# A K stage issued from a timetable instead of a loop: one pipelined stage of an attention and feed-forward kernel, reordered on four engines

## The chip, the cores and the metric

The kernel runs on one core of one Trainium2 chip. The metric is the device time of one execution in microseconds (us). Each execution is timed by itself; "fast" is the undisturbed state. The profiled execution of each kernel leaves a trace; its span is about 1.7 us shorter than the time of the same execution (530.5 against 532.15 us for the kernel before). PE is the matmul engine (TensorE), PEld its weight load, DVE the vector engine, ACT the scalar engine, POOL the general-purpose engine, SP the engine that issues the loads and stores here. "Landing" is the moment at which loaded data is there. A "bank" is a part of ps_all, the memory that PE's results go to; it can be written anew once DVE and ACT have read it.

## The reference, cut to what matters

```python
def _A_ref(x, wqkv, wo):                       # x: 1 x 2048 x 576, 32 heads of 18
    qkv = ((x @ wqkv).reshape(B, S, 3, H, Dh)).transpose(2, 0, 3, 1, 4)
    q, k, v = qkv[0], qkv[1], qkv[2]
    phi = lambda t: jnp.where(t > 0, t + 1, jnp.exp(t)) + 1e-6
    pq, pk = phi(q), phi(k)
    kv = jnp.einsum("bhsd,bhse->bhde", pk, v)
    z = jnp.einsum("bhsd->bhd", pk)
    ...                                        # num / den, then @ wo
def _B_ref(x, w_gate, w_up, w_down):
    return (_gelu(x @ w_gate) * (x @ w_up)) @ w_down
xn = _layernorm(x, axis=-1)
return x + _A_ref(xn, A_wqkv, A_wo) + _B_ref(xn, B_w_gate, B_w_up, B_w_down)
```

The sums over tokens in kv and z are taken on PE as a Gram matrix of xn and pk, so that V is never formed.

## The kernel before

The 2048 tokens are 16 tiles of 128. Each tile goes through a pipeline: statistics (mean and variance: DVE, two halves and an aggregate), rstd (one over the square root of the variance; ACT: Ln, then Exp), norm (DVE), five transposes (PE) and their copy (ACT), ten K matmuls in two halves (PE), phi of K (relu and exp on ACT, max on DVE, a sum on POOL), and the Gram matmuls two tiles behind (PE). In these traces each engine takes its instructions in the program's order: in experiment 4 ACT stands still for 0.99 us before one instruction while the input of a later one is ready.

```python
    def ln_rstd(n, cnt=1):
        r = rstd[:, n:n + cnt]
        nc.scalar.activation(out=r, in_=mv[:, n:n + cnt, 1], func=ACT.Ln, bias=eps_ln[:], scale=1.0)
        nc.scalar.activation(out=r, in_=r, func=ACT.Exp, scale=-0.5)
    ...
    for n in range(1, NS):                      # NS = 16, PAIRED = 7, GLAG = 2
        if n > 1:
            k_half(n, 0); k_half(n, 1)
        if n + 1 < NS:
            tp_all(n + 1)                       # ACT copies the transposes
        if n + 2 < NS and (n + 2 < PAIRED or n % 2 == 1):
            ln_rstd(n + 2, min(1 if n + 2 < PAIRED else 2, NS - n - 2))
        if n + 2 < NS:
            ln_norm(n + 2)
        k_read(n, 0); k_read(n, 1); k_finish(n) # relu, max; exp and POOL sum
        ln_stats(2 * (n + 4) + (1 if n < PAIRED - 4 else 2))   # half statistics done so far
        if n >= GLAG:
            g_accumulate(n - GLAG, G_A)
        if n + 2 < NS:
            transposes(n + 2)
        if n in (NS - 2, NS - 1):
            q_unit(...)                         # Q units 0 and 1 between the last K tiles
        ...                                     # loads of x and of later weights
    ...
    for i in range(2, NSC * NCH):               # the other Q units
        q_unit(i)
        if i < 2 + GLAG:
            g_accumulate(NS - GLAG + i - 2, G_A)    # the last two Gram tiles
        ...
```

The first two tiles have a hand-written order ahead of this loop. Q is made in units, each a block of five matmuls followed by its own phi. The phi tiles of K and of the Q units share one pool: three buffers for the exp side, two (phi_a) for the max side. After the Q units come the denominators, and from about 77 us on the feed-forward part, 85% of the time.

Of the kernel before, what the change touches and what calls it, by code (L numbers as in the profile page):

```python
# [8 lines left out]
ACT = mybir.ActivationFunctionType  # L9
# [6 lines left out]
P = 128  # L16
# [23 lines left out]
GLAG = 2  # L40
PAIRED = 7
XW = 642
# [14 lines left out]
def kernel(  # L57
# [139 lines left out]

    ln_done = [0]

    def ln_stats(halves):  # L200

        while ln_done[0] < min(halves, 2 * NS):
            n, a_ = divmod(ln_done[0], 2)
            if a_ == 0:
                stats_t[n] = asmall.tile([P, 2, nc.vector.BN_STATS_DIM], F32, name="stats")
            nc.vector.bn_stats(out=stats_t[n][:, a_, :], in_=x_sb[:, n, a_ * HALF:(a_ + 1) * HALF])
            if a_ == 1:
                nc.vector.bn_aggr(out=mv[:, n, :], in_=stats_t.pop(n)[:])
            ln_done[0] += 1

    def ln_rstd(n, cnt=1):
        r = rstd[:, n:n + cnt]
        nc.scalar.activation(out=r, in_=mv[:, n:n + cnt, 1], func=ACT.Ln, bias=eps_ln[:], scale=1.0)
        nc.scalar.activation(out=r, in_=r, func=ACT.Exp, scale=-0.5)

    def ln_norm(n, dup=None):
        nc.vector.tensor_scalar(  # L217
            out=xn[:, n, 0:D], in0=x_sb[:, n, :], scalar1=mv[:, n, 0:1], scalar2=rstd[:, n:n + 1],
            op0=ALU.subtract, op1=ALU.mult,
        )  # L220
        (dup or nc.gpsimd).tensor_copy(out=xn[:, n, D:640], in_=xn[:, n, 512:D])

# [5 lines left out]

    def tp_copy(n, k0, k1, copy):
        copy(out=xnT[:, k0:k1, n * P:(n + 1) * P], in_=tp_bank[:, k0:k1, :])  # L230

# [18 lines left out]

    def k_read(n, hf):
        if hf == 0:
            k_ea[n] = phi_tiles()
        e, a = k_ea[n]
        hs = slice(hf * HALF, (hf + 1) * HALF)
        src = ps_all[:, k_bank(n, hf), :HALF]
        nc.scalar.activation(out=e[:, hs], in_=src, func=ACT.Relu, scale=-1.0)
        nc.vector.tensor_scalar(
            out=a[:, hs], in0=src, scalar1=0.0, scalar2=EPS_ATT, op0=ALU.max, op1=ALU.add,
        )  # L260

    def k_finish(n):
        e, a = k_ea.pop(n)
        nc.scalar.activation(out=e[:], in_=e[:], func=ACT.Exp, scale=-1.0)  # L264
        nc.gpsimd.tensor_tensor(out=pk[:, n, :], in0=e[:], in1=a[:], op=ALU.add)  # L265
# [10 lines left out]
    def g_accumulate(n, pieces):  # L276
# [10 lines left out]
    G_COPIES = {  # L287
        3: [(0, G_A, 0, acopy), (0, G_A, 1, vcopy), (2, G_A, 0, acopy), (2, G_A, 1, vcopy)],
        5: [(1, G_A, 0, acopy), (2, G_A, 2, vcopy)],
# [3 lines left out]
    }  # L293

    def tp_all(n):
        tp_copy(n, 0, KT, acopy)

    q_next = [0]

# [86 lines left out]


    ln_stats(2)
    ln_rstd(0)
    ln_stats(3)  # L390
    ln_norm(0, nc.vector)
    transposes(0)
    ln_stats(4)
    tp_copy(0, 0, KT, vcopy)
    ln_rstd(1)
    k_half(0, 0)
    ln_norm(1)
    transposes(1)
    ln_stats(6)
    k_half(0, 1)  # L400
    k_read(0, 0)
    tp_all(1)
    ln_rstd(2)
    ln_stats(7)
    k_half(1, 0)
    ln_norm(2)
    k_read(0, 1)
    k_finish(0)
    transposes(2)
    k_half(1, 1)  # L410
    ln_stats(9)


    for n in range(1, NS):

        if n > 1:
            k_half(n, 0)
            k_half(n, 1)
        if n + 1 < NS:
            tp_all(n + 1)  # L420
        if n + 2 < NS and (n + 2 < PAIRED or n % 2 == 1):
            ln_rstd(n + 2, min(1 if n + 2 < PAIRED else 2, NS - n - 2))
        if n + 2 < NS:
            ln_norm(n + 2)
        k_read(n, 0)
        k_read(n, 1)
        k_finish(n)
        ln_stats(2 * (n + 4) + (1 if n < PAIRED - 4 else 2))
        if n >= GLAG:
            g_accumulate(n - GLAG, G_A)  # L430
        if n + 2 < NS:
            transposes(n + 2)
        if n in (NS - 2, NS - 1):
            q_unit(q_next[0])
            q_next[0] += 1
        if n == 2:
            load_x(8, 4)
        elif n == 3:
            load_x(12, 4)
        elif n == 5:  # L440
            load_w(0)
        elif n == 6:
            load_w(2)
        elif n == 7:
            load_wo()
        elif 8 <= n < 8 + NWBUF:
            load_gu(n - 8, 0)
            load_gu(n - 8, 1)

# [7 lines left out]
    for i in range(2, NSC * NCH):  # L457
        if i == 8:
            q_banks = _Ring([2, 3, 4, 5, 6, 7])
        q_unit(i)  # L460
        if i < 2 + GLAG:
            g_accumulate(NS - GLAG + i - 2, G_A)
        for kt, pieces, part, copy in G_COPIES.get(i, ()):
            g_copy(kt, pieces, part, copy)
        if i == 10:
            z_stage()
        if 5 <= i < 13:
            for n in (2 * (i - 5), 2 * (i - 5) + 1):
                g_accumulate(n, G_B)
        if 13 <= i < 13 + NCH:  # L470
            den_mm(0, i - 13, q_banks.next())
        if i == 17:
            kv_stage()
# [163 lines left out]
```

## Time and profile before

| what | kernel before |
|---|---|
| time, median of 3 (range) | 532.59 us (532.07 to 533.6) |
| span of the profiled run, granted clock | 530.5 us, 1.0 |
| K stage and Q units, up to the first feed-forward matmul | 77.66 us |
| feed-forward part, from there to the end | 452.8 us |
| K stage, per tile, tiles 5 to 13 | 2.625 us |

The change touches only the first 77 us, and what it does there is read off the moment at which the first feed-forward matmul starts. The chain of waits is the profile's account of what the last instruction waited for, followed back in time; its columns are start, length, what. That moment stands in the last line here:

```profile
75.47 2.18 PE ps_all L310 x10
77.66 1.40 PE ps_all L505 x11
```

L310 is the last Q unit, L505 the feed-forward part. The other lines of the profile before are in the prediction.

### The profile page before, as it was taken

To read this page: it belongs to the slowest core of one execution; us is meant where nothing else is said; L and a number is where in the kernel's file an instruction comes from. 1 tells how busy PE (TensorE), PEld (TensorE's weight loads), DVE (VectorE), ACT (ScalarE), POOL (GpSimd) and SP (SyncE) were. 2 spreads that over 40 slices of the span, in tenths; PEclk is the share of its full clock that TensorE was granted. 3 is DMA by queue.
4 is the path that set the end of the run, shared out by engine and by line. 5 is a ranking of instruction groups with operands and counts; after the bars stand their busy time and mean duration, and the time that the engine had idled before them with its cause. 6 is when DMAs were issued, how large, how long until landed. Compare 5 with 4: busy or idle time off the path is not lost.

```text
span 530.5 us, 10752 instructions
## 1 busy us (share of the span) xinstructions
PE 522.6 (99%) x4532; PEld 314.3 (59%) x4532; DVE 248.7 (47%) x408; ACT 152.5 (29%) x288; POOL 70.3 (13%) x83
## 2 busy tenths in 40 slices
PE   7999999999999999999999999999999999999997
PEld 5887666444467754444477744444677544445775
DVE  7885666783338613333368233333485143333101
ACT  6887783323330003323200022323100132322000
POOL 4666542110002100000012000000021000000000
PEclk9999999999999999999999999999999999999999
DMA  8910006898510025555400055555100345540000
GB/s 283 248 30 1 1 2 184 261 270 267 143 39 12 23 78 153 148 150 157 135 12 12 12 153 162 146 157 153 49 22 13 94 143 158 155 135 1 12 12 22
DMA packets 98810, 55.85 MB, mean 105 GB/s; under 512 B 5322, under 2 KB 98378, under 8 KB 98762
## 3 DMA queue, kind: packets, MB, share of 16 engines
q1 hardware_dynamic: 98762, 55.17, 36.2%
q8 instruction: 35, 0.57, 0.4%
q14 instruction: 13, 0.11, 0.1%
HBM read 52.79 MB, written 2.36 MB: 104 GB/s over the span
## 4 chain that ended last, share of the span: by engine, by line
PE 95%; SPq 2%; DVE 1%; ACT 1%; issue 0%; DMA 0%
PE ps_all L505 51%; PE ps_all L576 27%; PE ps_all L310 4%; PE ps_all L581 4%; PE ps_all L280 4%; PE ps_all L238 3%; PE ps_all L227 1%; SPq L166 1%; PE ps_all L370 1%; SPq L168 0%; SPq L169 0%; DMA x_sb<-in_A_x_dram 0%; ACT xnT L230 0%; DVE xn L217 0%; PE ps_all L358 0%
## 5 line engine op out<-in xcount | busy, mean ns | idle before, releaser
L505 PE MATMUL ps_all<-xnT,wg 64*128 64x512 bf16 x1152 | 274.1, 377 | 0.0
L505 PE MATMUL ps_all<-xnT,wu 64*128 64x512 bf16 x1152 | 272.6, 377 | 0.9 <-SPq L514 0.3
L549 DVE TENSOR_TENSOR hT<-ps_all,gl 128x512 bf16<-128x512 f32 x144 | 99.6, 692 | 168.9 <-ACT gl L548 168.7
L548 ACT ACTIVATE gl<-ps_all 128x512 f32<-128x512 f32 x144 | 86.0, 597 | 316.7 <-PE ps_all L505 294.9
L505 PEld LDWEIGHTS <-wu 64*128 64x128 bf16 x1152 | 106.9, 94 | 70.9 <-SPq L514 8.7
L505 PEld LDWEIGHTS <-wg 64*128 64x128 bf16 x1152 | 107.0, 94 | 66.7 <-issue 0.3
L576 PE MATMUL ps_all<-wd_sb,hT 128*128 128x288 bf16 x1152 | 146.6, 286 | 0.0
L576 PEld LDWEIGHTS <-hT 128*128 128x128 bf16 x1152 | 112.2, 98 | 31.5 <-issue 1.9
L384 DVE RECIPROCAL den_sb<-den_sb 126x128 f32<-126x128 f32 (+1 forms) x80 | 68.3, 911 | 0.5
L385 POOL TENSOR_TENSOR pqT<-pqT,den_sb 126x512 bf16<-126x512 bf16 (+3 forms) x25 | 24.1, 965 | 301.5 <-DVE den_sb L384 298.2
L584 DVE TENSOR_TENSOR res<-ps_all,x_sb 128x288 bf16<-128x288 f32 x32 | 14.6, 458 | 88.3 <-PE ps_all L581 88.3
L505 PE MATMUL ps_all<-xnT,wr 64*128 64x512 bf16 x288 | 55.9, 377 | 0.0
L581 PE MATMUL ps_all<-m_sb,pqT 126*128 126x288 bf16 (+1 forms) x160 | 24.9, 286 | 0.0
L505 PEld LDWEIGHTS <-wr 64*128 64x128 bf16 x288 | 14.6, 94 | 17.4 <-issue 1.1
L310 PE MATMUL ps_all<-xnT,wqkv_sb 128*126 128x512 bf16 (+1 forms) x100 | 24.4, 380 | 0.0
L265 POOL TENSOR_TENSOR hT<-phi_e,phi_a 128x576 bf16<-128x576 f32 x16 | 22.5, 1404 | 8.9 <-ACT phi_e L264 4.9
L280 PE MATMUL ps_all<-hT,xn 128*128 128x288 bf16 (+3 forms) x192 | 23.6, 266 | 0.0
L238 PE MATMUL ps_all<-wqkv_sb,xnT 128*128 128x288 bf16 x160 | 22.4, 286 | 0.8 <-DVE xnT L230 0.6
L280 PEld LDWEIGHTS <-xn 128*128 128x128 bf16 (+1 forms) x192 | 18.2, 101 | 4.5
L320 POOL TENSOR_TENSOR pqT<-phi_e,phi_a 126x512 bf16<-126x512 f32 (+1 forms) x14 | 17.7, 1268 | 15.5 <-DVE phi_a L318 11.8
L581 PEld LDWEIGHTS <-pqT 126*128 126x128 bf16 (+1 forms) x160 | 15.5, 97 | 4.1
L238 PEld LDWEIGHTS <-xnT 128*128 128x128 bf16 x160 | 15.0, 98 | 4.5 <-DVE xnT L230 0.8
(58 smaller groups left out, 200.6 us busy)
## 6 DMA issues: line engine op xcount, KB each, us to landing
wg<-in_B_w_gate_dram SPq DMA_DIRECT2D x72, 256.0 KB, 2.9
wu<-in_B_w_up_dram SPq DMA_DIRECT2D x72, 256.0 KB, 3.4
wd_sb<-in_B_w_down_dram SPq DMA_DIRECT2D x12, 432.0 KB, 4.5
wr<-in_B_w_gate_dram SPq DMA_DIRECT2D x72, 32.0 KB, 2.7
wr<-in_B_w_up_dram SPq DMA_DIRECT2D x72, 32.0 KB, 3.1
out_dram<-res SPq DMA_DIRECT2D x15, 144.0 KB, 1.8
x_sb<-in_A_x_dram SPq DMA_DIRECT2D x3, 576.0 KB, 6.6
wqkv_sb<-in_A_wqkv_dram SPq DMA_DIRECT2D x2, 576.0 KB, 9.2
```

The costliest lines, as they stand in the source:

```text
L238: nc.tensor.matmul(ps_all[:, k_bank(n, hf), :HALF], lhsT=xnT[:, kt, n * P:(n + 1) * P], rhs=wqkv_sb[:, kt, D + hf * HALF:D + (hf + 1) * HALF],
L265: nc.gpsimd.tensor_tensor(out=pk[:, n, :], in0=e[:], in1=a[:], op=ALU.add)
L280: nc.tensor.matmul(ps_all[:m, b, col:col + w], lhsT=xn[:, n, j0:j0 + m], rhs=pk[:, n, d0:d0 + w], start=(n == 0 and col == 0), stop=(n == ...
L310: nc.tensor.matmul(ps, lhsT=wqkv_sb[:, kt, q0:q0 + rows], rhs=xnT[:, kt, cs], start=(kt == 0), stop=(kt == KT - 1),)
L320: nc.gpsimd.tensor_tensor(out=pqT[:rows, c, cs], in0=e, in1=a, op=ALU.add)
L384: nc.vector.reciprocal(out=d[:, h:h + P], in_=d[:, h:h + P])
L385: nc.gpsimd.tensor_tensor(out=pqT[:rows, c, cols], in0=pqT[:rows, c, cols], in1=d, op=ALU.mult)
L505: return nc.tensor.matmul(self.outs[i], lhsT=self.lhs(i, rows, kt), rhs=self.rhs(i, rows, kt), start=start, stop=stop, skip_group_check=True,)
L548: nc.scalar.activation(out=gl[:], in_=ps_all[:, b[0], :], func=ACT.Gelu_apprx_tanh)
L549: nc.vector.tensor_tensor(out=hT[:, GUB * k + i, :], in0=ps_all[:, b[1], :], in1=gl[:], op=ALU.mult)
L576: nc.tensor.matmul(acc, lhsT=hT[:, f, j * P:(j + 1) * P], rhs=wd_sb[:, f, hs], start=(f == 0), stop=False,)
L581: nc.tensor.matmul(acc, lhsT=pqT[:rows, c, ts_], rhs=m_sb[:rows, c, hs], start=False, stop=(c == NCH - 1),)
```

## The change

The loop is replaced by a table. Each step of a tile has a list of times, the first four tiles with times of their own, later tiles 2.5 us apart; all steps are sorted by time and issued in that order. Three things come with it. No rstd is paired any more. Inside a tile the second K half stands after the next tile's transposes, and the halves' statistics, relus and maxes are issued one by one. At the end, Q unit 0 stands ahead of K of tile 15, and the last two Gram tiles, the copies that read them and the second Gram pass move one Q unit later. The times in the table fix only an order; nothing waits for a clock.

```diff
-PAIRED = 7
...
+    TILE = 2.5
+    STEPS = [
+        (lambda n: ln_half(n, 0), [3.02, 3.99, 6.44, 7.41, 9.44]),
+        (lambda n: ln_half(n, 1), [3.51, 4.48, 6.93, 7.90, 9.93]),
+        (ln_rstd, [4.14, 5.11, 7.56, 10.12, 11.84]),
+        (ln_norm, [4.96, 5.69, 8.38, 10.77, 12.80]),
...
+        (transposes, [5.66, 6.57, 9.14, 11.53, 13.62]),
+        (tp_copy, [6.07, 6.98, 9.56, 12.27, 14.12]),
+        (lambda n: k_half(n, 0), [6.86, 8.09, 10.30, 13.01, 15.56]),
+        (lambda n: k_half(n, 1), [7.47, 9.43, 10.91, 13.91, 16.46]),
...
+        (lambda n: k_max(n, 0), [8.72, 10.41, 12.44, 14.61, 17.27]),
+        (lambda n: k_max(n, 1), [9.08, 11.11, 13.28, 15.60, 17.84]),
+        (k_exp, [8.73, 11.12, 13.29, 15.61, 18.10]),
+        (k_add, [9.59, 11.73, 14.01, 16.29, 19.88]),
+    ]
+    G_AT = [11.82, 14.53, 17.07, 19.62, 22.16]
+    todo = [(at(times, n), step, n) for n in range(NS) for step, times in STEPS]
+    todo += [(at(G_AT, n), lambda n: g_accumulate(n, G_A), n) for n in range(NS - GLAG)]
+    todo += [(at(STEPS[7][1], NS - 1) - 0.01, q_unit, 0), (at(G_AT, NS - GLAG) - 0.01, q_unit, 1)]
+    for _, step, n in sorted(todo, key=lambda x: x[0]):
+        step(n)
...
-        if i < 2 + GLAG:
-            g_accumulate(NS - GLAG + i - 2, G_A)
+        if 3 <= i < 3 + GLAG:
+            g_accumulate(NS - GLAG + i - 3, G_A)
```

More of the change, by code (lines that the diff above doesn't have):

```diff
@@ L196, with ln_half, ln_rstd, ln_norm @@
     stats_t = {}
-    ln_done = [0]
-    def ln_stats(halves):
-        while ln_done[0] < min(halves, 2 * NS):
-            n, a_ = divmod(ln_done[0], 2)
-            if a_ == 0:
-                stats_t[n] = asmall.tile([P, 2, nc.vector.BN_STATS_DIM], F32, name="stats")
-            nc.vector.bn_stats(out=stats_t[n][:, a_, :], in_=x_sb[:, n, a_ * HALF:(a_ + 1) * HALF])
-            if a_ == 1:
-                nc.vector.bn_aggr(out=mv[:, n, :], in_=stats_t.pop(n)[:])
-            ln_done[0] += 1
-    def ln_rstd(n, cnt=1):
-        r = rstd[:, n:n + cnt]
-        nc.scalar.activation(out=r, in_=mv[:, n:n + cnt, 1], func=ACT.Ln, bias=eps_ln[:], scale=1.0)
+    def ln_half(n, a_):
+        if a_ == 0:
+            stats_t[n] = asmall.tile([P, 2, nc.vector.BN_STATS_DIM], F32, name="stats")
+        nc.vector.bn_stats(out=stats_t[n][:, a_, :], in_=x_sb[:, n, a_ * HALF:(a_ + 1) * HALF])
+        if a_ == 1:
+            nc.vector.bn_aggr(out=mv[:, n, :], in_=stats_t.pop(n)[:])
+    def ln_rstd(n):
+        r = rstd[:, n:n + 1]
+        nc.scalar.activation(out=r, in_=mv[:, n, 1:2], func=ACT.Ln, bias=eps_ln[:], scale=1.0)
         nc.scalar.activation(out=r, in_=r, func=ACT.Exp, scale=-0.5)
-    def ln_norm(n, dup=None):
+    def ln_norm(n):
         nc.vector.tensor_scalar(
@@ L220, in ln_norm, with ln_dup @@
         )
-        (dup or nc.gpsimd).tensor_copy(out=xn[:, n, D:640], in_=xn[:, n, 512:D])
+    def ln_dup(n):
+        (nc.gpsimd if n else nc.vector).tensor_copy(out=xn[:, n, D:640], in_=xn[:, n, 512:D])
     tp_bank = ps_all[:, 7, :].bitcast(BF16).rearrange("p (k t) -> p k t", t=P)
@@ L227, in transposes, with tp_copy @@
             nc.tensor.transpose(tp_bank[:, kt, :], xn[:, n, kt * P:(kt + 1) * P], ident[:])
-    def tp_copy(n, k0, k1, copy):
-        copy(out=xnT[:, k0:k1, n * P:(n + 1) * P], in_=tp_bank[:, k0:k1, :])
+    def tp_copy(n):
+        copy = acopy if n else vcopy
+        copy(out=xnT[:, :, n * P:(n + 1) * P], in_=tp_bank[:, 0:KT, :])
     def k_bank(n, hf):
@@ L249, with k_relu, k_max, k_exp @@
     k_ea = {}
-    def k_read(n, hf):
+    def k_relu(n, hf):
         if hf == 0:
             k_ea[n] = phi_tiles()
-        e, a = k_ea[n]
         hs = slice(hf * HALF, (hf + 1) * HALF)
-        src = ps_all[:, k_bank(n, hf), :HALF]
-        nc.scalar.activation(out=e[:, hs], in_=src, func=ACT.Relu, scale=-1.0)
+        nc.scalar.activation(out=k_ea[n][0][:, hs], in_=ps_all[:, k_bank(n, hf), :HALF], func=ACT.Relu, scale=-1.0)
+    def k_max(n, hf):
+        hs = slice(hf * HALF, (hf + 1) * HALF)
         nc.vector.tensor_scalar(
-            out=a[:, hs], in0=src, scalar1=0.0, scalar2=EPS_ATT, op0=ALU.max, op1=ALU.add,
-        )
-    def k_finish(n):
+            out=k_ea[n][1][:, hs], in0=ps_all[:, k_bank(n, hf), :HALF],
+            scalar1=0.0, scalar2=EPS_ATT, op0=ALU.max, op1=ALU.add,
+        )
+    def k_exp(n):
+        e = k_ea[n][0]
+        nc.scalar.activation(out=e[:], in_=e[:], func=ACT.Exp, scale=-1.0)
+    def k_add(n):
         e, a = k_ea.pop(n)
-        nc.scalar.activation(out=e[:], in_=e[:], func=ACT.Exp, scale=-1.0)
         nc.gpsimd.tensor_tensor(out=pk[:, n, :], in0=e[:], in1=a[:], op=ALU.add)
@@ L287 @@
     G_COPIES = {
-        3: [(0, G_A, 0, acopy), (0, G_A, 1, vcopy), (2, G_A, 0, acopy), (2, G_A, 1, vcopy)],
+        4: [(0, G_A, 0, acopy), (0, G_A, 1, vcopy), (2, G_A, 0, acopy), (2, G_A, 1, vcopy)],
         5: [(1, G_A, 0, acopy), (2, G_A, 2, vcopy)],
@@ L293 @@
     }
-    def tp_all(n):
-        tp_copy(n, 0, KT, acopy)
-    q_next = [0]
     q_banks = _Ring([7])
@@ L385, in den_norm @@
         nc.gpsimd.tensor_tensor(out=pqT[:rows, c, cols], in0=pqT[:rows, c, cols], in1=d, op=ALU.mult)
-    ln_stats(2)
-    ln_rstd(0)
-    ln_stats(3)
-    ln_norm(0, nc.vector)
-    transposes(0)
-    ln_stats(4)
-    tp_copy(0, 0, KT, vcopy)
-    ln_rstd(1)
-    k_half(0, 0)
-    ln_norm(1)
-    transposes(1)
-    ln_stats(6)
-    k_half(0, 1)
-    k_read(0, 0)
-    tp_all(1)
-    ln_rstd(2)
-    ln_stats(7)
-    k_half(1, 0)
-    ln_norm(2)
-    k_read(0, 1)
-    k_finish(0)
-    transposes(2)
@@ L410 @@
-    k_half(1, 1)
-    ln_stats(9)
-    for n in range(1, NS):
-        if n > 1:
-            k_half(n, 0)
-            k_half(n, 1)
-        if n + 1 < NS:
-            tp_all(n + 1)
-        if n + 2 < NS and (n + 2 < PAIRED or n % 2 == 1):
-            ln_rstd(n + 2, min(1 if n + 2 < PAIRED else 2, NS - n - 2))
-        if n + 2 < NS:
-            ln_norm(n + 2)
-        k_read(n, 0)
-        k_read(n, 1)
-        k_finish(n)
-        ln_stats(2 * (n + 4) + (1 if n < PAIRED - 4 else 2))
-        if n >= GLAG:
-            g_accumulate(n - GLAG, G_A)
-        if n + 2 < NS:
-            transposes(n + 2)
-        if n in (NS - 2, NS - 1):
-            q_unit(q_next[0])
-            q_next[0] += 1
-        if n == 2:
-            load_x(8, 4)
-        elif n == 3:
-            load_x(12, 4)
-        elif n == 5:
-            load_w(0)
-        elif n == 6:
-            load_w(2)
-        elif n == 7:
-            load_wo()
-        elif 8 <= n < 8 + NWBUF:
-            load_gu(n - 8, 0)
-            load_gu(n - 8, 1)
+    TILE = 2.5
@@ new lines @@
+    STEPS = [
[3 more added lines that the diff above has]
+        (ln_norm, [4.96, 5.69, 8.38, 10.77, 12.80]),
+        (ln_dup, [5.43, 6.16, 8.85, 11.24, 13.27]),
+        (transposes, [5.66, 6.57, 9.14, 11.53, 13.62]),
+        (tp_copy, [6.07, 6.98, 9.56, 12.27, 14.12]),
+        (lambda n: k_half(n, 0), [6.86, 8.09, 10.30, 13.01, 15.56]),
+        (lambda n: k_half(n, 1), [7.47, 9.43, 10.91, 13.91, 16.46]),
+        (lambda n: k_relu(n, 0), [7.99, 9.28, 11.56, 13.84, 16.55]),
+        (lambda n: k_relu(n, 1), [8.27, 10.55, 12.83, 15.11, 17.39]),
+        (lambda n: k_max(n, 0), [8.72, 10.41, 12.44, 14.61, 17.27]),
[3 more added lines that the diff above has]
+    ]
@@ new lines, with at @@
+    G_AT = [11.82, 14.53, 17.07, 19.62, 22.16]
+    def at(times, n):
+        return times[n] if n < len(times) else times[-1] + TILE * (n - len(times) + 1)
+    todo = [(at(times, n), step, n) for n in range(NS) for step, times in STEPS]
+    todo += [(at(G_AT, n), lambda n: g_accumulate(n, G_A), n) for n in range(NS - GLAG)]
+    todo += [(at(STEPS[7][1], NS - 1) - 0.01, q_unit, 0), (at(G_AT, NS - GLAG) - 0.01, q_unit, 1)]
+    load_x(8, 4)
+    load_x(12, 4)
+    load_w(0)
+    load_w(2)
+    load_wo()
@@ L451, in g_copy @@
+    for i in range(NWBUF):
+        load_gu(i, 0)
+        load_gu(i, 1)
+    for _, step, n in sorted(todo, key=lambda x: x[0]):
+        step(n)
     def g_copy(kt, pieces, part, copy):
@@ L466 @@
             z_stage()
-        if 5 <= i < 13:
-            for n in (2 * (i - 5), 2 * (i - 5) + 1):
+        if 6 <= i < 14:
+            for n in (2 * (i - 6), 2 * (i - 6) + 1):
                 g_accumulate(n, G_B)
```

## The prediction

> **What bounds the kernel now.** The page's first lines are read first: which engine is busy, and what the chain that ended last is made of.
>
> ```profile
> PE 522.6 (99%) x4532; PEld 314.3 (59%) x4532; DVE 248.7 (47%) x408; ACT 152.5 (29%) x288; POOL 70.3 (13%) x83
> ...
> PE 95%; SPq 2%; DVE 1%; ACT 1%; issue 0%; DMA 0%
> ```
>
> The kernel is TensorE from end to end; the change adds and removes no matmul, so it can only win TensorE gaps. Its busy figure hides small waits, so I read the K stage in two ways. By stretch of time (columns: length, then us of busy time and instruction counts of PE, PEld, DVE, ACT, POOL, then the granted clock, DMA share and GB/s):
>
> ```profile
> 5.00:10.00 5.00, 4.12 (x38) 2.72 (x36) 4.50 (x15) 3.12 (x9) 0.61 (x3) 1.00 0.99 354
> 10.00:15.00 5.00, 3.94 (x40) 3.06 (x38) 4.21 (x12) 4.87 (x13) 3.33 (x5) 1.00 1.06 368
> 15.00:20.00 5.00, 5.00 (x53) 4.28 (x51) 4.62 (x16) 4.80 (x13) 3.28 (x5) 1.00 1.13 219
> 20.00:30.00 10.00, 10.00 (x98) 8.14 (x96) 8.66 (x24) 8.47 (x20) 6.37 (x8) 1.00 0.77 201
> ```
>
> Here PE lacks some 2 us before 15 us, and DVE and ACT are both near full: three engines are almost balanced. From 15 to 20 us there are 53 matmuls in 5 us, from 20 to 30 us only 98 in 10: the steady state got slower although PE still shows as full. The timeline says why. The change to look for is the first instruction that idles:
>
> ```profile
> 20.42 0.21 DVE L208 BATCH_NORM_AGGREGATE mv<-stats 128x2 f32<-128x12 f32 x1
> ...
> 20.67 0.30 ACT L213 ACTIVATE rstd<-mv,eps_ln 128x2 f32<-128x2 f32 x1 [0.42 <-DVE mv L208]
> 21.00 0.21 ACT L214 ACTIVATE rstd<-rstd 128x2 f32<-128x2 f32 x1
> ...
> 21.24 0.43 DVE L217 TENSOR_SCALAR xn<-x_sb,mv,rstd 128x576 bf16<-128x576 bf16 x1 [0.61 <-ACT rstd L214]
> ...
> 21.72 0.40 PEld L227 LDWEIGHTS <-xn 128*128 128x128 bf16 x5 [0.19 <-DVE xn L217]
> ```
>
> From tile 7 on, one rstd serves two tiles, so it waits for the second tile's statistics; ACT, then DVE, then the transposes wait in a row. The first K matmuls of tiles 3, 4, 5, 6, 7, 8, 9 start at 14.36, 16.84, 19.36, 22.12, 24.65, 27.41 and 29.90 us: 2.48 and 2.52 us per tile with single rstds, then 2.76 + 2.53 and 2.76 + 2.49. Over the eight tiles from 5 (19.36) to 13 (40.36) it is 21.00 us, 2.625 each. From tile 13 to the feed-forward part at 77.6 us PE has no gap.
>
> **What the Trainium skill says.** "TensorE: Matmul & The Clock Gate", Back-to-back issue gap, gives N/2.4 + 2.5 ns between warm matmuls, though it warns that streams with weight loads may differ. For one tile that is 5 x 55.8 (transposes) + 10 x 122.5 (K) + (2304 columns / 2.4 + 10 x 2.5) (Gram) = 0.28 + 1.23 + 0.98 = 2.49 us. This trace agrees: the chain of waits has exactly pieces of 0.28, 1.23 and 0.98 us, and single-rstd tiles take 2.49. So 2.49 is the floor per tile and TILE = 2.5 sits on it. "Perfetto Trace Analysis", Optimizing Scalar/DVE Operations, says that grouping into larger operations helps a saturated engine; pairing rstd was that. The trace agrees with the saving (0.30 us for two columns as for one) and shows its price, the wait above. "PSUM — Partial Sum Buffer", PSUM bank collisions, asks for semaphores per bank between readers; the built program has them (each DVE max waits for the ACT relu of the same bank), and the tail below turns on that.
>
> **The change, part by part.**
>
> *Single rstd for tiles 7 to 14.* Four more Ln/Exp pairs, about 0.44 us of ACT each. ACT per tile is then: relu 0.30, relu to exp 0.42, exp 0.59, copy 0.69, Ln to Exp 0.33, Exp 0.11, as issue distances in the timeline around 16 us: 2.44 us, just under 2.49. If PE holds its floor over the eight tiles: 21.00 - 8 x 2.49 = **1.08 us gained**. I trust this most, because tiles 3 to 5 of the kernel before already ran so.
>
> *The first four tiles.* The timetable wants the K matmuls of tile 4 at 15.56 us; before, they stand at 16.84, after one transpose group more (0.28), so at equal work 16.56: 1.0 us on paper. But the new order puts both halves of the statistics of tiles 2 and 3 ahead of norm 2 on DVE, at 6.44 and 7.41, and the landings in the trace are about 6.85 us for x of tile 2 and 8.1 for tile 3 (tile 4's block 9.5). DVE works in order, so I replay it with row durations (statistics 0.41 a half, aggregate 0.16 with its wait, norm 0.43, max 0.41): tile 2's statistics 6.85 to 7.67; tile 3's 8.1 to 8.92; norm 2 at 9.1 (before 8.80); two maxes, tile 4's statistics, one max, norm 3 at 11.7 (before 11.01); norm 4 at 13.9 (before 13.38); norm 5 at 16.1 (before 15.87). On PE: transposes 2 at 9.55, both K halves of tile 2 from 10.85, transposes 3 at 12.2, Gram 0 at 12.6, K of tile 3 at 13.55, then with waits of 0.2 on norm 4 and on the bank, K of tile 4 at about 16.35. The split of K around the transposes fills most of the old 1.06 us hole before tile 3's transposes, and DVE's late start takes most of that back: gain 0.2 by replay, 1.0 by timetable. I take **0.4 us**.
>
> *Q unit 0 ahead of K of tile 15, and the Gram tail.* In the built order the POOL sum of Q unit 0 now stands ahead of the K sum of tile 14, and ACT does Q 0's relu and exp before tile 14's exp. Before:
>
> ```profile
> 46.41 0.60 ACT L317 ACTIVATE phi_e<-ps_all 126x512 f32<-126x512 f32 x1 [1.01 <-PE ps_all L310]
> 47.04 0.63 ACT L319 ACTIVATE phi_e<-phi_e 126x512 f32<-126x512 f32 x1
> ...
> 48.31 1.27 POOL L320 TENSOR_TENSOR pqT<-phi_e,phi_a 126x512 bf16<-126x512 f32 x1 [1.43 <-ACT phi_e L257]
> ```
>
> In the new order the first DVE max of tile 15 waits for that POOL sum (its phi_a buffer is the one Q 0 had; two buffers). Count from the first K matmul of tile 14: Q 0 on PE at 2.45; its relu 1.35 later as before (46.41 against 45.06), 3.8; max 0.70 later, 4.5 to 5.2; POOL sum 5.35 to 6.6; tile 15's first max 6.65 to 7.1. Q unit 2 wants that bank on PE at 6.8 (0.60 + 0.28 + 0.60 + 0.98 + 1.08 + 1.23 + 0.98 + 1.08): a new wait of 0.3 us, or 0.7 if the POOL sum is again 0.4 us later than its inputs (48.31 against 47.80 + 0.14). Gram 15 needs POOL's sum of tile 15: Q 1's sum 8.9 to 10.15, then 1.40 to 11.55, against PE's arrival at 11.4 with the tail one Q unit later (without that shift at 10.3, a wait of over 1 us; so the shift is needed by the new order and gains nothing against before). **Cost 0.5 us.**
>
> *The loads* stand in the same order on their queue: 0.
>
> Sum: 1.08 + 0.4 - 0.5 = 1.0 us of 532.6. After the stage PE has no gap for the rest of the run, so what is won at 50 us arrives at the end whole.
>
> **The rivals.**
>
> *The timetable works as written:* landings early enough, no new wait in the tail: 1.0 + 1.08 = 2.1 us, 530.5. For it: the times fit the engines' row durations. Against: the landings above and the POOL order.
>
> *ACT becomes the bound of the steady state.* 2.44 us of work against 2.49; every tile now has five separate waits on PE in ACT's queue. If each tile slips to 2.55, the gain falls by 0.5 us. For it: ACT shows 4.80 of 5 us busy between 15 and 20 us. Against: the K matmuls need ACT only through the copy of the transposes, which is some 0.6 us early.
>
> *The tail costs more:* POOL chain 0.4 late twice, and the queue of DVE behind it holds Q 5: 1.5 us lost, total about 0 (532.6).
>
> *Hidden anyway:* not possible here; PE is gapless afterwards, and the weights for the feed-forward part lie in SBUF by 30 us.
>
> **Range and chances.** Central 532.59 - 1.0 = 531.6 us. The rivals span 530.5 to 532.6; the kernel before itself varied from 532.07 to 533.6 over three runs, so I widen by some 0.2 us below and 0.3 above: 530.3 to 532.9. Two per cent is 10.7 us; the whole stage has under 4 us of PE waits to win and no step that could cost ten: 1 per cent faster, 98.5 same, 0.5 slower.
>
> **What would show it.** Right: K of tiles 5 to 13 spaced 2.49 us; no two-column rstd; DVE idle on x before tile 2's or 3's statistics; norm 3 later than 11.0 us; PE waiting for a DVE max between Q unit 1 and Q unit 2; the first feed-forward matmul near 76.6 us instead of 77.6. Wrong: tiles at 2.55 or more (ACT), K of tile 4 near 15.6 (landings did not matter), no wait at Q 2, or a first feed-forward matmul that moved without the end moving.

## The result, and the profile after

| | before | after |
|---|---|---|
| median of 6 runs (range), same rounds | 532.33 us (531.39 to 533.6) | 531.42 us (530.73 to 532.01) |
| span of the profiled run | 530.5 us | 529.7 us |
| first feed-forward matmul | 77.66 us | 76.67 us |
| from there to the end | 452.8 us | 453.0 us |

The ratio is 0.9982, 95% interval 0.9967 to 0.9996. A ratio here is the mean time of one kernel's fast runs over that of the other's of the same rounds, so not quite the ratio of the medians. That is about 1.0 us, as predicted, and far inside the 2% that count as the same.

The end of the chain of waits up to the feed-forward part (now L479), for the kernel after:

```profile
74.48 2.18 PE ps_all L306 x10
76.67 2.48 PE ps_all L479 x21
```

It is 0.99 us earlier, and the part behind it is as long as before within 0.2 us. The page's first lines do not show such a change; DVE and POOL have the same count, ACT the eight instructions (four Ln, four Exp) of the four added rstds:

```profile
PE 521.6 (98%) x4532; PEld 311.3 (59%) x4532; DVE 246.9 (47%) x408; ACT 153.6 (29%) x296; POOL 70.3 (13%) x83
```

The same stretches as in the prediction, for the kernel after (columns as there):

```profile
5.00:10.00 5.00, 3.39 (x34) 2.35 (x32) 4.17 (x14) 3.11 (x9) 0.47 (x2) 1.00 0.94 319
10.00:15.00 5.00, 4.69 (x45) 3.63 (x45) 4.77 (x14) 4.84 (x14) 3.54 (x5) 1.00 1.05 375
15.00:20.00 5.00, 5.00 (x53) 4.31 (x51) 4.14 (x12) 4.76 (x14) 3.41 (x5) 1.00 1.13 249
20.00:30.00 10.00, 10.00 (x103) 8.62 (x101) 8.30 (x24) 9.55 (x26) 6.59 (x9) 1.00 0.77 198
```

From 20 to 30 us PE starts 103 matmuls where it started 98, with the same "busy" 10.00: the count shows what the busy share hides. ACT is now busy for 9.55 of 10 us (8.47 before). From 5 to 10 us PE does less than before (34 for 38), from 10 to 15 more (45 for 40).

A tile of the steady state in the chain of waits, for the kernel after:

```profile
18.88 0.61 PE ps_all L234 x5
19.50 0.28 PE ps_all L222 x5
19.77 0.61 PE ps_all L234 x5
20.39 0.98 PE ps_all L281 x10
21.37 0.61 PE ps_all L234 x5
```

K half, transposes, K half, Gram, and 2.49 us later the next tile's K half. Nothing but PE is in it, and this holds from tile 4 to tile 13.

The waits of PE from 8 us to the end of the Q units (columns: what was waited for, us in total, times, longest), first of the kernel before, then of the kernel after. The view leaves out short gaps; the waits at the tail, below, are not in it.

```profile
PE ps_all L227 <- DVE xn L217: 1.1, 1, 1.1
PE ps_all L238 <- DMA wqkv_sb<-in_A_wqkv_dram: 0.2, 1, 0.2
```

```profile
PE ps_all L222 <- DVE xn L210: 0.4, 1, 0.4
PE ps_all L234 <- DMA wqkv_sb<-in_A_wqkv_dram: 0.2, 1, 0.2
PE ps_all L234 <- ACT xnT L226: 0.2, 1, 0.2
```

The 1.1 us hole before tile 3's transposes is gone, and smaller ones stand in its place. What opens them is in DVE's timeline, for the kernel after:

```profile
6.92 0.82 DVE L200 BATCH_NORM_STATS2 stats<-x_sb 128x6 f32<-128x288 bf16 x2 [0.40 <-DMA x_sb<-in_A_x_dram]
...
8.22 0.82 DVE L200 BATCH_NORM_STATS2 stats<-x_sb 128x6 f32<-128x288 bf16 x2 [0.23 <-DMA x_sb<-in_A_x_dram]
...
9.20 0.38 DVE L210 TENSOR_SCALAR xn<-x_sb,mv,rstd 128x576 bf16<-128x576 bf16 x1
```

Twice DVE idles until x lands, and norm 2 (9.20) stands behind tile 3's statistics. K of tile 4 starts at 16.23 us. Before it was 16.84 with one group of transposes more done, so 16.56 at equal work: 0.33 us are won by the first tiles. At tile 13 the gap has grown: K starts at 38.63 against 40.36 - 0.28 = 40.08, so 1.45 us, of which 1.12 came from the steady state (1.09 of it from tile 5 to tile 13, the stretch that the prediction counts: 21.00 against 19.91). At the end only 0.99 is left, so the tail gave 0.46 back. It is one wait and a little at the last Gram tile; the timeline of the kernel after:

```profile
46.50 1.27 POOL L316 TENSOR_TENSOR pqT<-phi_e,phi_a 126x512 bf16<-126x512 f32 x1 [3.07 <-DVE phi_a L314]
...
47.81 0.82 DVE L255 TENSOR_SCALAR phi_a<-ps_all 128x288 f32<-128x288 f32 x2 [1.45 <-POOL pqT L316]
```

DVE's max of tile 15 waits 1.45 us for POOL's sum of Q unit 0, which held the phi_a buffer. Q unit 1 ends on PE at 48.00, and the bank that Q unit 2 needs is freed at 48.28, by the first of these two maxes: PE starts at 48.32. The chain of waits has this, and in its last line here Gram tile 15, which takes 1.13 us where a Gram tile without a wait takes 0.98:

```profile
47.81 0.47 DVE phi_a L255
...
48.32 2.32 PE ps_all L306 x10
...
52.70 1.13 PE ps_all L281 x10
```

### The profile page after: what moved, and what is told of

It is laid out like the page before. It is cut to its first block, busy times and chain, and to the rows that moved or that the text cites. A ratio compares the mean times of both kernels' runs of the same rounds, so it can differ in the third digit from the quotient of the medians.

```text
span 529.7 us, 10752 instructions
## 1 busy us (share of the span) xinstructions
PE 521.6 (98%) x4532; PEld 311.3 (59%) x4532; DVE 246.9 (47%) x408; ACT 153.6 (29%) x296; POOL 70.3 (13%) x83
## 4 chain that ended last, share of the span: by engine, by line
PE 93%; SPq 3%; DVE 1%; DMA 1%; issue 0%; POOL 0%; ACT 0%; DVEq 0%; POOLq 0%; ACTq 0%
PE ps_all L479 51%; PE ps_all L550 27%; PE ps_all L306 4%; PE ps_all L555 4%; PE ps_all L281 3%; PE ps_all L234 3%; PE ps_all L366 1%; DMA x_sb<-in_A_x_dram 1%; SPq L165 1%; SPq L168 1%; PE ps_all L222 1%; SPq L167 0%; DVE phi_a L255 0%; DVE stats L200 0%; SPq L92 0%
## 5 line engine op out<-in xcount | busy, mean ns | idle before, releaser
L479 PE MATMUL ps_all<-xnT,wu 64*128 64x512 bf16 x1152 | 273.5, 376 | 0.9 <-SPq L488 0.5
L479 PE MATMUL ps_all<-xnT,wg 64*128 64x512 bf16 x1152 | 274.0, 376 | 0.0
L479 PEld LDWEIGHTS <-wu 64*128 64x128 bf16 x1152 | 106.9, 94 | 72.7 <-SPq L488 9.4
L479 PEld LDWEIGHTS <-wg 64*128 64x128 bf16 x1152 | 106.9, 94 | 67.8
L479 PE MATMUL ps_all<-xnT,wr 64*128 64x512 bf16 x288 | 54.7, 376 | 0.0
L234 PE MATMUL ps_all<-wqkv_sb,xnT 128*128 128x288 bf16 x160 | 24.3, 286 | 0.6 <-DMA wqkv_sb<-in_A_wqkv_dram 0.2
L479 PEld LDWEIGHTS <-wr 64*128 64x128 bf16 x288 | 14.0, 94 | 17.7 <-issue 1.1
L255 DVE TENSOR_SCALAR phi_a<-ps_all 128x288 f32<-128x288 f32 x32 | 14.2, 450 | 7.1 <-ACT phi_e L251 5.6
```

What stands on the lines that cost most here:

```text
L234: nc.tensor.matmul(ps_all[:, k_bank(n, hf), :HALF], lhsT=xnT[:, kt, n * P:(n + 1) * P], rhs=wqkv_sb[:, kt, D + hf * HALF:D + (hf + 1) * HALF],
L479: return nc.tensor.matmul(self.outs[i], lhsT=self.lhs(i, rows, kt), rhs=self.rhs(i, rows, kt), start=start, stop=stop, skip_group_check=True,)
```

## The experiments

All eleven gave correct results. The times of single runs of one kernel spread by 0.7 to 3 us, about as much as what is looked for or more, so beside the ratio I read each trace: when K of tile 3 starts (the first tiles are over), when the feed-forward part starts, and the time between. That difference takes the first tiles out of the comparison. Each kernel has one trace, and the landings differ from trace to trace.

| run | second K weights / x of tile 3 landed | K of tile 3 | first feed-forward matmul | between | ratio to before (95%) |
|---|---|---|---|---|---|
| after | 7.82 / 8.19 | 13.74 | 76.67 | 62.93 | 0.9982 (0.9967 to 0.9996) |
| 1 single_rstd | 7.67 / 8.03 | old order | 76.66 | | 0.9967 (0.9953 to 0.998) |
| 2 k14_first | 8.12 / 8.50 | 14.06 | 76.52 | 62.46 | 0.9957 (0.9943 to 0.997) |
| 3 tail_early | 8.11 / 8.54 | 14.10 | 78.08 | 63.98 | 1.0000 (0.9985 to 1.0015) |
| 4 dve_order | 7.67 / 8.06 | 14.44 | 77.92 | 63.48 | 0.9991 (0.9976 to 1.0006) |
| 5 x_first | 8.45 / 6.59 | 14.11 | 77.03 | 62.92 | 0.9984 (0.9969 to 0.9999) |
| 6 k14_x_first | 8.23 / 6.84 | 13.89 | 76.36 | 62.47 | 0.9994 (0.9975 to 1.0014) |
| 7 first_tiles | 7.85 / 8.22 | 13.77 | 78.37 | 64.60 | 1.002 (1.0003 to 1.0038) |
| 8 rstd_x_first | 8.12 / 6.51 | old order | 76.85 | | 0.9986 (0.9972 to 1.0) |
| 9 pairs_lead | 7.76 / 8.15 | 14.00 | 76.47 | 62.47 | 0.9972 (0.9955 to 0.9989) |
| 10 old_pairs_lead | 7.39 / 7.76 | old order | 77.74 | | 0.9994 (0.998 to 1.0008) |
| 11 norm2_first | 7.71 / 8.09 | 14.12 | 76.59 | 62.47 | 0.9972 (0.9958 to 0.9987) |

Theory: the change gains on PE what the single rstd no longer makes it wait (1.08 us) and a little in the first tiles, and pays 0.5 us at the tail through POOL's order. Rivals: the timetable as a whole is what gains; the tail is free; the first tiles could gain much more if one wait were removed.

**1. The single rstd alone.** The kernel before with one constant changed.

```diff
-PAIRED = 7
+PAIRED = 18
```

> The kernel before with one constant changed: every tile has its own rstd (no pairs), nothing else moved. Theory (pairs cost 0.26 us each): K matmuls of tiles 5 to 13 spaced 2.49 us, first feed-forward matmul 1.1 us earlier than in the kernel before (77.66 to about 76.55 us), time about 0.998 of before. Rival (the gain comes from the new step order, and four more rstds on a full ACT cost as much as the pairs): spacing 2.55 or more, first feed-forward matmul less than 0.5 us earlier.

Measured: 531.27 us against 533.23, ratio 0.9967. The first feed-forward matmul is at 76.66, and all tiles from 3 on are 2.49 apart. One constant in the old order gives as much as the whole change. It follows that the rest of the change, first tiles and tail, came to about nothing in sum.

**2. Tile 14's POOL sum ahead of Q unit 0's.** The kernel after, with only this order changed. In the table STEPS[7] is the first K half; below, STEPS[0] and STEPS[1] are the two statistics halves.

```diff
+    moved = {(k_add, 14): 43.105, (STEPS[7][0], 15): 43.107, (k_add, 15): 47.14}
+    todo = [(moved.get((step, n), t), step, n) for t, step, n in todo]
-    todo += [(at(STEPS[7][1], NS - 1) - 0.01, q_unit, 0), ...
+    todo += [(43.106, q_unit, 0), ...
```

> The changed kernel, but tile 14's exp on ACT and its sum on POOL stand ahead of Q unit 0's, and tile 15's sum ahead of Q unit 1's; PE's order is untouched. Theory (the new PE wait of 0.3 us between Q units 1 and 2 and that of 0.15 us before Gram 15 come from that order): both waits gone, first feed-forward matmul at about 76.2 us instead of 76.67. Rival (PE waits for something else there, for instance DVE being late with the maxes): the waits stay, 76.6 or later.

Measured: 530.67 us, ratio 0.9957, the lowest of all. The waits at Q unit 2 and at Gram tile 15 are gone, and the stretch from K of tile 3 to the feed-forward part is 62.46 us instead of 62.93: the tail cost 0.47 us, as the prediction had it. The same two places in its chain of waits, PE without a break:

```profile
47.39 3.25 PE ps_all L306 x15
...
52.71 0.98 PE ps_all L281 x10
```

The first feed-forward matmul came at 76.52 and not at the expected 76.2, because the first tiles were 0.32 us late in this run: x of tile 3 landed at 8.50 instead of 8.19. This is the version that beats both kernels; against the kernel before it is shown, against the kernel after only the traces and the ratios of different rounds speak for it. Experiment 1 ran in the same rounds: 531.27 us (530.97 to 531.67) against 530.67 (530.24 to 531.35) here. The ranges overlap, and the first feed-forward matmul is only 0.14 us earlier, so a gain of the timetable over that one constant is not clear of the noise.

**3. The Gram tail back at its old units.** The kernel after with the last Gram tiles, their copies and the second Gram pass one Q unit earlier again.

```diff
-        if 3 <= i < 3 + GLAG:
-            g_accumulate(NS - GLAG + i - 3, G_A)
+        if 2 <= i < 2 + GLAG:
+            g_accumulate(NS - GLAG + i - 2, G_A)
```

> The changed kernel with the Gram tail, its copies and the second Gram part back at the Q units of the kernel before. Theory (the shift is needed by the new POOL order): PE waits about 1.1 us before Gram 15 for POOL's sum of tile 15, first feed-forward matmul near 77.7 us, the gain of the change used up. Rival (the shift does nothing): 76.7 us, no wait before Gram 15.

Measured: 532.78 us, ratio 1.0000; the stretch is 63.98, so 1.05 us more than after. The timeline of this kernel has the wait:

```profile
53.04 1.15 PE L281 MATMUL ps_all<-hT,xn 128*128 128x288 bf16 x10 [1.05 <-POOL hT L266]
```

PE arrives at Gram tile 15 before POOL has summed tile 15. So "Gram tail one Q unit later" is no gain by itself: it is what the new POOL order makes necessary, and without it the change would be worth nothing.

**4. Another order on DVE in tiles 2 to 6.** Norm 3 earlier, later statistics behind it.

```diff
-        (lambda n: ln_half(n, 1), [3.51, 4.48, 6.93, 7.90, 9.93]),
+        (lambda n: ln_half(n, 1), [3.51, 4.48, 6.93, 8.50, 10.70, 13.40, 14.93]),
-        (ln_norm, [4.96, 5.69, 8.38, 10.77, 12.80]),
+        (ln_norm, [4.96, 5.69, 8.38, 10.13, 12.80]),
...                                             # statistics' first halves and two maxes too
```

> The changed kernel with another DVE order for tiles 2 to 6: the second half of tile 3's statistics after norm 2, tile 4's second half after tile 1's maxes, tile 5's statistics after norm 4. Theory (in the first tiles DVE is the bound, in order behind the landing of tile 3's x at 8.2 us): norm 2 at about 8.7 us instead of 9.20, K of tile 4 at 15.7 to 15.9 us instead of 16.23, first feed-forward matmul 0.3 to 0.5 us earlier than 76.67. Rival (the first tiles are bound by ACT or by the K weights' landing): norm 2 earlier, but K of tile 4 stays within 0.1 us of 16.23.

A miss of both sides: ratio 0.9991, K of tile 4 at 16.94, K of tile 3 at 14.44, 0.70 us later than after, and a further 0.55 us lost by the end of the stage (63.48 against 62.93), at tiles 5 and 8, which come 2.82 and 2.70 us behind the ones before them. Its timeline:

```profile
13.27 0.30 ACT L206 ACTIVATE rstd<-mv,eps_ln 128x1 f32<-128x1 f32 x1 [0.99 <-DVE mv L202]
...
13.71 0.67 ACT L226 COPY xnT<-ps_all 128x640 bf16<-128x640 bf16 x1
...
14.44 0.79 PE L234 MATMUL ps_all<-wqkv_sb,xnT 128*128 128x288 bf16 x5 [0.74 <-ACT xnT L226]
```

I had moved tile 4's statistics later on DVE; ACT has rstd 4 ahead of the copy of tile 3's transposes, so it stood still for 0.99 us with that copy behind it, and PE waited. DVE is thus not the only queue that sets the first tiles; ACT's order hands a late statistic of one tile to the copy of another. The block of x with tile 4 landed at 10.48 us here and 9.66 in the run after, so part of this miss is the landing. The runs separate the two: experiment 9 has the order of the run after in the first tiles and landings within 0.1 us of these (x of tile 3 at 8.15 and 8.06, the block at 10.53 and 10.48), and its K of tile 3 starts at 14.00. By that comparison 0.44 us of the 0.70 are the order and 0.26 the landing.

**5. x ahead of the K weights.** The kernel after with x of tiles 2 and 3 each one place earlier in the load queue; **6.** the same with the edit of experiment 2.

```diff
+    load_x(2, 1)
     load_wk(0)
     nc.sync.dma_start(wqkv_sb[0:HP, 4, D:2 * D], ...)
-    load_x(2, 1)
-    load_wk(1)
     load_x(3, 1)
+    load_wk(1)
```

> The kernel after, with x of tile 2 queued ahead of the first K weights and x of tile 3 ahead of the second. Theory (the landing of x of tile 3, 8.19 us, sets norm 2 and with it the first tiles): x of tile 2 lands near 5 and tile 3 near 7.3 us, norm 2 starts near 8.3 us instead of 9.20, while the second K half of tile 0 waits longer (its weights near 8.3 instead of 7.82); transposes 2 near 8.9, K of tile 3 starts at 13.2 to 13.4 instead of 13.74, first feed-forward matmul 76.2 to 76.4 instead of 76.67, time 0.3 to 0.5 us below the kernel after. Rival (the K weights, 0.5 us later, cost what x gains, or the block of tiles 4 to 7 is later): K of tile 3 at 13.7 or later, first feed-forward matmul 76.7 or later.

> The kernel after with both edits: sum of tile 14 ahead of Q unit 0 in POOL's queue (no wait at Q 2 and Gram 15), and x of tiles 2 and 3 queued ahead of the K weights. If both theories hold they add: first feed-forward matmul at 75.8 to 76.0 us, time about 530.4, some 1.9 us under the kernel before. Rival: the load order gains nothing, then 76.2 to 76.5 as with the first edit alone.

The rival was right for the first: x of tile 3 landed 1.60 us earlier and norm 2 started at 8.34 instead of 9.20, as expected, and it was worth nothing. K of tile 3 came at 14.11. PE waited elsewhere; this is its timeline in experiment 5:

```profile
8.49 1.39 PE L234 MATMUL ps_all<-wqkv_sb,xnT 128*128 128x288 bf16 x10 [0.86 <-DMA wqkv_sb<-in_A_wqkv_dram]
```

The second K weights landed at 8.45 instead of 7.82. ACT's relu of that K half stood ahead of its copy of the next transposes, so K of tile 2 waited another 0.59 us. Together the two edits of experiment 6 gave 62.47 for the stretch, the tail gain again, and 76.36 for the feed-forward start, the earliest of all, where its rival had it (76.2 to 76.5); its time (531.75 median, ratio 0.9994) does not show it, its runs going from 530.3 to 533.25 us.

**7. The timetable with paired rstds.** What the first four tiles are worth alone: the kernel of experiment 2, with rstds of tiles 7 to 14 paired again, each pair placed right after the second tile's statistics.

```diff
     def ln_rstd(n):
-        r = rstd[:, n:n + 1]
+        if n > 7 and n % 2 == 0:
+            return
+        cnt = 2 if 7 <= n < NS - 1 else 1
+        r = rstd[:, n:n + cnt]
```

> The timetable of the first four tiles alone: the kernel after with the paired rstd of tiles 7 to 14 put back (each pair after the second tile's statistics) and without the wait at Q 2. Theory (single rstd is worth 0.135 us a tile over eight tiles, whatever the order): K matmuls alternate 2.76 and 2.49 us from tile 7, first feed-forward matmul 1.08 us later than the same kernel with single rstds, at 77.3 to 77.6 us; so the first tiles alone gain 0.1 to 0.35 us against 77.66 of the kernel before, and the time is 0.1 to 0.35 us below it. Rival (in the timetable's order the pair's wait is hidden, since statistics stand earlier ahead of the norm): spaced 2.49 throughout, first feed-forward matmul 76.2 to 76.5.

A miss, later than either side expected: 532.99 us, ratio 1.002. The stretch is 64.60 us, 2.14 more than the same order with single rstds, where the old order had lost only 1.0 to 1.1 by pairing. From tile 6 on the tiles alternate 3.02 and 2.49, not 2.76 and 2.49: two take 5.51. Its chain of waits no longer runs over PE alone:

```profile
20.14 0.46 DVE phi_a L258
20.59 0.38 DVE stats L200
...
20.99 0.22 DVE mv L202
...
21.24 0.31 ACT rstd L209
...
21.81 0.44 DVE xn L213
...
22.29 0.53 PE ps_all L225 x5
```

In the timetable's order the second tile's last half statistic stands behind the max of the K half that PE has just finished, and the pair waits for both. A single rstd uses statistics done one tile's time earlier. So the new order depends on single rstds more than the old one did, and the two parts of the change do not simply add.

**8. x first in the old order.** Experiment 1 with the load order of experiment 5.

> The kernel before with single rstds (PAIRED = 18) and x of tiles 2 and 3 queued ahead of the K weights. In this order norm 2 stands ahead of tile 3's statistics, so only x of tile 2 counts and the copy of transposes 2 follows K of tile 0. Theory (x landings bound the timetable, not the old order): K weights 0.5 us later push the old order's first tiles later or leave them, first feed-forward matmul 76.6 to 77.1 instead of 76.66. Rival (x bounds both): 76.2 to 76.4.

Measured: ratio 0.9986, first feed-forward matmul 76.85 instead of 76.66. As expected, the old order wins nothing from x. That the later K weights cost the 0.2 us is not shown: K of tile 3 starts at 14.66 here, and at 14.36, 14.48 and 14.77 in the three runs of the old order with the old loads (before, 1 and 10).

**9. Pairs with a lead.** Is it pairing that costs, or where the statistics stand? Experiment 7, with the second tile's last half statistic moved ahead of the max that it stood behind (0.5 us in the table, one place in DVE's queue).

```diff
+        moved[STEPS[1][0], n + 1] = at(STEPS[0][1], n + 1) + 0.001
-        moved[ln_rstd, n] = at(STEPS[1][1], n + 1) + 0.01
+        moved[ln_rstd, n] = at(STEPS[0][1], n + 1) + 0.002
```

> As the run of the first tiles alone (timetable, paired rstd of tiles 7 to 14, no wait at Q 2), but the second tile's last half statistic is moved up by 0.5 us in the timetable, ahead of the max that it stood behind, and the pair's rstd with it. Theory (a pair costs what its norm waits for the second tile's statistics, and nothing by itself): the pair's rstd is done about 1 us ahead of the norm, K spaced 2.49 us throughout, first feed-forward matmul near 76.5 (that of the same kernel with single rstds), 1.8 us earlier than the 78.37 of the run without the lead. Rival (pairing costs time as such, as a longer chain over ACT): over 5.2 us per two tiles, first feed-forward matmul 77.3 or later.

Confirmed: 531.09 us, ratio 0.9972, tiles 2.49 us apart throughout, stretch 62.47 us, the same as with single rstds (62.46). Pairing costs nothing; a pair whose second input is late costs 2.1 us over the stage. The lead was smaller than expected: the pair's rstd ended 0.03 us before its norm, not 1 us, and DVE idled 0.40 us for it; PE did not, since the transposes came later still. From the timeline:

```profile
20.37 0.21 DVE L202 BATCH_NORM_AGGREGATE mv<-stats 128x2 f32<-128x12 f32 x1
...
20.50 0.41 DVE L258 TENSOR_SCALAR phi_a<-ps_all 128x288 f32<-128x288 f32 x1
20.73 0.31 ACT L209 ACTIVATE rstd<-mv,eps_ln 128x2 f32<-128x2 f32 x1
...
21.31 0.43 DVE L213 TENSOR_SCALAR xn<-x_sb,mv,rstd 128x576 bf16<-128x576 bf16 x1 [0.40 <-ACT rstd L210]
```

The aggregate now stands ahead of the max, and rstd runs beside it.

**10. Pairs with a lead in the old order.** The kernel before, statistics going up to one tile further ahead from tile 7 on.

```diff
-        ln_stats(2 * (n + 4) + (1 if n < PAIRED - 4 else 2))
+        ln_stats(2 * (n + 4) + (1 if n < PAIRED - 4 else min(4, n - 1)))
```

> The kernel before with PAIRED left at 7, and statistics running one tile further ahead from tile 7 on (three half statistics per tile until the lead is there). Theory (same): the pair no longer waits, K spaced 2.49 us instead of 2.76 and 2.49, first feed-forward matmul about 1.0 us earlier than 77.66, so 76.6 to 76.8, time near that of the single rstd (0.9967 of before). Rival: pairing as such costs: spaced as before, 77.5 or later.

Half right. From tile 7 to tile 14 K is 2.49 apart, pairs or not. But the first feed-forward matmul is at 77.74, and the ratio is 0.9994. From tile 7 to tile 13 the stage won 0.77 us (14.94 against 15.71). While the lead was built up, with three half statistics per tile, DVE fell behind: from tile 5 to tile 7 it took 5.73 us instead of 5.29, so 0.44 of this was lost again. The rest went at the start: K of tile 5 came at 19.78 against 19.36, and K of tile 4, up to which the order is that of the kernel before, was already as late (17.26 against 16.84); so this part is not the lead's. In this order the lead cost over half of what it won; in experiment 9 it was only a place in the queue.

**11. Norm 2 ahead of tile 3's statistics.** Experiment 2 with this one move.

```diff
+    moved.update({(STEPS[0][0], 3): 8.385, (STEPS[1][0], 3): 8.386})
```

> The kernel after with tile 14's sum first (as in the first run of that) and with one more edit: norm 2 ahead of the statistics of tile 3 on DVE, nothing else moved. Theory (norm 2 stands behind statistics that wait for x of tile 3): norm 2 at 8.2 to 8.5 us instead of 9.2 to 9.5, transposes 2 at 9.3 directly behind the K half of tile 1, K of tile 3 at 13.3 to 13.6 instead of 13.74 to 14.06, first feed-forward matmul 75.9 to 76.2, some 0.3 to 0.4 us under 76.52 after allowing for the landings. Rival (what norm 2 gains, norm 3 loses, as its statistics come later): K of tile 3 earlier but K of tile 4 at the same time or later, 76.5 or more.

The rival was right: norm 2 at 8.58, transposes 2 at 9.07, but K of tile 3 at 14.12 and the feed-forward part at 76.59. DVE now idles 0.60 us for rstd 2, where it idled 0.23 for x; the work ahead of norm 3 is the same in either order, and norm 3 starts at 11.88 instead of 11.51 (the run after, with landings within 0.15 us of these). In the eight runs of the timetable other than experiment 4, K of tile 3 starts between 13.74 and 14.12 us. Five of them have the same order in the first tiles (after, 2, 3, 7 and 9) and span 13.74 to 14.10 by themselves. What differs are the landings: in 2 and 3 x of tile 3 came at 8.50 and 8.54, and in 9 DVE idled 0.30 us for the block of x with tile 4, which came at 10.53. No move of a load, a norm or a statistic brought it lower: with each, another of DVE, ACT and the K weights became what PE waited for. The timetable's own 13.01 stayed out of reach.

## Why the prediction was right

The sum was +1.08 for the rstds, +0.4 for the first tiles, -0.5 for the tail. The traces give +1.12, +0.33 and -0.46, which is the 0.99 us by which the feed-forward part starts earlier; the time fell by 0.0018 of 532.33, so 0.96 us.

*Single rstd.* Right in size and sign: tiles 5 to 13 are 2.49 us apart (1.09 us won over the stretch that was to give 1.08), no rstd has two columns. Experiment 1 gives the same gain alone, and experiment 9 shows the cause that the prediction named, the wait for the second tile's statistics: with that input early, pairs cost nothing. What it did not see is that the size belongs to the order: 1.0 to 1.1 us in the old one, 2.14 in the timetable's.

*First tiles.* The replay of DVE's queue was good to 0.3 us: norm 2 at 9.20 (9.1), norm 3 at 11.51 (11.7), norm 4 at 13.61 (13.9), norm 5 at 16.11 (16.1), K of tile 4 at 16.23 (16.35). The choice of 0.4 between 0.2 and 1.0 was a judgement, and that 0.33 came is in part luck: before and after are one trace each, whose landings happen to agree within 0.1 us. In the three traces of the old order with these loads K of tile 4 starts at 16.84 to 17.26 us, in the five of the new one at 16.23 to 16.59. The means, with 0.28 for the transposes, are 0.32 us apart, but single pairs give from -0.03 to 0.75. The reason given, that DVE's late start on x takes most of it back, is only half of it: with x early (experiment 5) nothing was won, since the K weights and ACT's queue come next.

*Tail.* Right: PE waited 0.32 us between Q units 1 and 2 for the max behind POOL's sum (predicted 0.3 or 0.7), and some 0.15 us at Gram tile 15. Experiment 2 removes both and gets 0.47 us back; experiment 3 gives the wait of 1.05 us which the prediction expected without the shift ("over 1 us").

*The loads and the rest.* "After the stage PE has no gap for the rest of the run" was too strong, and the weights for the feed-forward part do not all "lie in SBUF by 30 us": hardly anything is loaded from 30 to 80 us, but from 80 to 130 us the loads run at 166 to 275 GB/s again in the kernel before. The feed-forward part took 451.8 to 453.4 us over the thirteen traces of the same code, and the waits of PE on the load queue in it came to 0 to 0.8 us: none in the three shortest, 0.8 in the longest. Why experiment 6, earliest at 76.36 us, has a median of 531.75 us is not shown: its traced run, at 530.30 us, was the fastest of its six, with a feed-forward part of 452.2 us. Two of the others, at 532.06 and 533.25 us, had a granted clock of 0.997, where every other run in this document had 0.999 or more. For before and after the two parts happen to be alike (452.8 and 453.0), so the gain arrived whole.

*Rivals.* ACT did not become the bound of the steady state, though it is busy 9.55 of 10 us: the tiles hold 2.49. The timetable did not work as written (K of tile 4 planned at 15.56). The tail did not cost 1.5.

What stays open: POOL's sum of Q unit 0 starts about 0.5 us after the later of its inputs, where 0.14 us is usual, in the kernel before and in experiment 2, where the profile puts its wait down to a relu of tile 15, and not in the kernel after. And the landings were never held fixed: with them one order alone spreads K of tile 3 over 0.36 us. Experiments 4 and 11 can be read against a trace with like landings (9 and after). Experiments 5 and 6 change the landings on purpose and end within 0.01 us of that spread, so that x first is worth nothing is shown only to within 0.36 us.

## What to carry to other kernels

In a stage where one engine works without gaps, count its instructions per stretch of time and its spacing per tile; the busy share stays at 100% while a tile goes from 2.49 to 2.76 us. A grouped operation was free here when its last input was early and took the whole chain with it when it was late, so before ungrouping it look at what stands ahead of that input in its queue. With several queues about equally full, a new order here moved the wait rather than removing it: replay each in-order queue with the durations of the trace, and trust that more than the table of times the order was made from.

## What the Trainium skill lacked or had wrong

- "TensorE: Matmul & The Clock Gate", Back-to-back issue gap: it calls N/2.4 + 2.5 ns the isolated gap, and gives about 81 ns per matmul at N = 128 and 131 ns at N = 512 for sustained streams with weight loads. In this kernel's streams, each matmul with a weight load of its own, the formula holds and those figures do not: 0.28 us for five transposes (56 ns each), 0.61 us for five K matmuls of 288 columns (122 ns), 1.08 us for five Q matmuls of 512 columns (216 ns). The prediction's 2.49 us per tile was an estimate from that formula, for a stream all the same; the pieces of the trace give it too.
- "Perfetto Trace Analysis", Optimizing Scalar/DVE Operations: it advises grouping if the engine is saturated, and breaking up instructions if it is not but causes bubbles elsewhere. It lacks the third way, and the price: the same grouped rstd cost 0 or 2.14 us over eight tiles, according to whether the last input stood one place earlier in DVE's queue (experiments 9 and 7).
- "SBUF — State Buffer", SBUF: two separate sides: it says that a two-port DVE operation and a POOL operation lock each other out whole, and these traces agree, but it has no duration for a DVE operation behind a POOL one. The norm takes 0.38 to 0.43 us alone. In the thirteen traces 75 norms began while a sum of POOL ran. Of these 61 ended 0.16 to 0.18 us after the sum's end, whenever they had begun, and took up to 0.90 us (experiment 4: norm 11.00 to 11.90, sum 10.32 to 11.72). The other 14 began in the last 0.2 us of the sum and took 0.38 to 0.43 us, as alone.
- None of the pages named here has the spread from run to run: in the ten traces with the same load order the second K weights landed at 7.39 to 8.12 us, x of tile 3 at 7.76 to 8.54 and the four-tile block of x at 9.57 to 10.64, and the same feed-forward part took 451.8 to 453.4 us in all thirteen.
